# Heads by parity on the row halves, a four-block score product of 80 columns and a two-block one of 32

## Chip, cores and metric

The kernel runs on one core of a Trainium2 chip. The metric is the time of the whole program in microseconds (us) on that core. Everything is computed in float32.

## What is computed

```python
B, H, S, D = q.shape                         # 4, 8, 768, 48
mag = np.sqrt(a_re * a_re + a_im * a_im)
scale = np.minimum(mag, 0.999) / (mag + 1e-06)
a_re_n, a_im_n = (a_re * scale, a_im * scale)
for t in range(S):
    ...                                      # complex decay of the state S, then
    S_re, S_im = (new_re + kv, new_im)       # kv = outer(k_t, v_t)
    y[:, :, t] = q_t @ S_re
x = y.transpose(0, 2, 1, 3).reshape(B * S, H * D)    # 3072 x 384
h = np.maximum(np.maximum(x @ w1, x @ w2), x @ w3)   # 384 -> 768
return h @ w_out                                     # 768 -> 384
```

The recurrence is a gated linear attention with a complex decay for every head, step and feature. The kernel does it in tiles of 128 steps, each of two time chunks of 64: inside a chunk as a 64x64 lower-triangular matrix of scores per head, across chunks through a 48-feature complex state (96 rows of numbers, which lie in 112 rows: cosine parts in rows 0 to 47, nothing in 48 to 63, sine parts in 64 to 111).

## The kernel before

**Tiles.** A tile x is one sequence, 128 steps and all 8 heads; there are 24. Two tiles (two sequences, the same steps) make a group; there are 12. A tile's k, q and v lie as [128 rows, 2 chunks, 4 heads, 48]: rows 0 to 63 are the 64 steps of a chunk for heads 0 to 3, rows 64 to 127 the same steps for heads 4 to 7.

**Stages of a tile.** `gate_steps` and `angles` (ScalarE, VectorE, a little GpSimd) make the log-decays, cumulated phases, cosines and sines. `products` multiplies k and q by decay and phase into `uk` and `uq` (L471, L476, L481). `turn` transposes both with 16 matmuls against the identity, 64 rows at a time, and copies the results from PSUM on ScalarE into K (L495) and Q (L499). `cut` makes decay factors `f` at block borders: 16 small matmuls by a matrix of cuts, then four exponentials on ScalarE (L512 to L519). `prep` multiplies copies of K and Q by factors of f on VectorE (L527). `scores` makes two products on TensorE: A (K blocks of 32 keys x 48 columns of Q: the 32 queries of the block, and 16 more that carry a factor) and B (KB blocks of 32 keys x 80 columns of QB). `gather` assembles the 64x64 score matrices `atm` on VectorE with copies under a mask (L575): two from A, three from B. `state` carries the state on (`dk` on TensorE, L625 and L626 on VectorE). `outputs` sums "v times scores" and "state times q" into `y`, 32 output rows at a time, so that four runs go to four column strips of the array. Its result `xT` (L651) is what the feed-forward layer reads.

**Feed-forward.** `up_step` runs three weight matrices over 256 tokens and takes the maximum (L667, L669); `out_step` makes the 384 output columns and stores them (L677, L679).

**Layouts the change touches.** `vb` holds v as pairs of heads in 128 columns with a gap (a head in columns 0 to 47, the next in 80 to 127); each row half fills only its own four heads' slots and zeros stand in the others. So a 128-row product "v times scores" of two neighbouring heads' 32-row runs sees one head at a time: four runs of 32 for a pair, of which the two middle ones add into the same output strip. `g` (the state) has the same pairs. `uk` and `uq` have 128 columns per head.

**What sets the order.** TensorE's order is written out by hand from group 2 on: `chained` (L114) ties each matmul to the one before it in the source. ScalarE's table functions are tied in source order by `tab`. Everything else is ordered on each engine by the framework's planner, which lists instructions when it expects their inputs; the lists are fixed when the program is built. That it departs from the source can be seen in the trace. All loads and stores are issued on SP's queue. PSUM is a ring of four tiles of two banks (`banks`, L127), so a matmul group can wait for the reader of the tile four groups earlier.

In a group, after the first two tiles' prologue, the source order is:

```python
pairs(x)                     # scores A, B; gather A, B
turned(y)                    # turn k, q; cut; state; uk *= En; prep 0
outputs(x, tokens(x)); rest(y)
turning()                    # angles of the next group
pairs(y); units...; later    # uk, uq of the next group; gates of the one after it
turned(y + 1); outputs(y, tokens(y)); rest(y + 1)
```

with feed-forward steps of the tiles before fed in between by `feed`.

Of the kernel before, what the change touches and what calls it, by code (L numbers as in the profile page):

```python
# [51 lines left out]
def kernel(  # L52
# [31 lines left out]
    C8, C8B, C16, C32, CK, CG, CD, NF = 0, 4, 8, 12, 20, 28, 36, 37  # L84
# [83 lines left out]
    masko = const.tile([P, 4, 32], U8, name="masko")  # L168
# [4 lines left out]
    vbs = [const.tile([P, 2, H // 2, P], FP, name="vb%d" % i) for i in range(4)]  # L173
# [3 lines left out]
    us = {nm: [const.tile([P, H, 2, L64], FP, name="u%s%d" % (nm, i)) for i in range(n)] for nm, n in (("k", 3), ("q", 2))}  # L177
    fs = [const.tile([P, H, 2, NF], FP, name="f%d" % i) for i in range(2)]
    KB = const.tile([P, H, P], FP, name="KB")

    def constants_early():
# [11 lines left out]
        for o in (0, L64):  # L193
            def col(base, n):
                return cuts[o:o + L64, base:base + n]

            between(col(C8, 4), 7, 11, [[16, 4]], [[16, 4]])
            between(col(C8B, 4), 3, 7, [[16, 4]], [[16, 4]])
            vw = col(C16, 4).rearrange("p (n u) -> p n u", u=2)
            between(vw, 15, 19, [[32, 2], [0, 2]], [[32, 2], [8, 2]])  # L200
            vw = col(C32, 8).rearrange("p (i n) -> p i n", i=2)
            between(vw, 15, 35, [[16, 2], [0, 4]], [[0, 2], [8, 4]])
            vw = col(CK, 8).rearrange("p (n u) -> p n u", u=2)
            between(vw, 3, 15, [[16, 4], [8, 2]], [[16, 4], [0, 2]])
            between(col(CG, 8), -1, 3, [[0, 8]], [[8, 8]])

    def constants_late():
# [4 lines left out]
        f = nat1.tile([P, 4, 2, L64], FP, tag="e", padded_shape=[P, 6, 2, L64], name="maskf")  # L212
# [5 lines left out]
        g = f.rearrange("p i c t -> p (i c t)")[:, 0:4 * L64].rearrange("p (i t) -> p i t", i=4)  # L218
        nc.gpsimd.memset(g, 1.0)
        for i, h in enumerate((8, 16, 32, 32)):  # L220
            n, w = L64 // h, h if i < 2 else 16
            o = 16 if i == 3 else 0
            m = g[:, i].rearrange("p (n h) -> p n h", h=h)
            keep(m, -o, [[-2 * h, n], [0, h]], 1)
            keep(m, o + w - 1, [[2 * h, n], [0, h]], -1)
# [21 lines left out]
    def halves(a, g, c, j):  # L247
# [3 lines left out]
        return a[b * C + c, j * 4:(j + 1) * 4, t0:t0 + P, :].rearrange("h (c t) d -> t c h d", c=2)  # L251
# [8 lines left out]
    def load_v(g, c):  # L260
        x = g * C + c
        T["v", x] = vbs[x % 4]
        for j in range(2):
            src = halves(v, g, c, j).rearrange("t c (i u) d -> t c i u d", u=2)
            dst = T["v", x][j * L64:(j + 1) * L64, :, 2 * j:2 * j + 2]
            for ch in range(2):
                for u in range(2):
                    nc.sync.dma_start(out=heads(dst[:, ch])[:, :, u], in_=src[:, ch, :, u])
# [122 lines left out]
    def turns(g, cs, meanwhile):  # L391
# [8 lines left out]
        for c in cs:  # L400
            ps = banks("cs", DM)

            for ch in range(2):
                for j in range(2):
                    at = c * DM + j * HC
                    mm(out=ps[j * L64:(j + 1) * L64, ch * HC:(ch + 1) * HC], lhsT=upto[:, ch * L64:(ch + 1) * L64],
                       rhs=w[:, at:at + HC], start=True, stop=True)
# [7 lines left out]
            if (g + 1) % NS > 0:  # L415
                if c == 0:
                    T["carry", g + 1] = nat1.tile([1, W], FP, tag="carry", name="carry")
                for j in range(2):
                    last, at = (j + 1) * L64, c * DM + j * HC
                    nc.sync.dma_start(out=T["carry", g + 1][:, at:at + HC], in_=nf[last - 1:last, HC:])  # L420
# [20 lines left out]
    def both(t, h):  # L441

        return t[:, h].rearrange("p u d -> p (u d)")[:, 0:DD]
# [7 lines left out]
    def products(x):  # L451
        g, c = divmod(x, C)

        def s0():
# [3 lines left out]
            for n, mat in enumerate((mid, rest)):  # L458
                for j in range(2):
                    for ch in range(2):  # L460
                        r = slice(ch * L64, (ch + 1) * L64)
                        at = c * DM + j * HC
                        mm(out=ps[j * L64:(j + 1) * L64, ch, n * HC:(n + 1) * HC], lhsT=mat[r],
                           rhs=T["Ln", g][r, at:at + HC], start=True, stop=True)
# [8 lines left out]
        def s1():  # L473
            for nm in "kq":
                u = T["U" + nm, x] = us[nm][x % len(us[nm])]
                nc.vector.tensor_tensor(out=u[:, :, :, 0:D], in0=T["CS", x], in1=two(hd(T[nm, x])), op=OP.mult)  # L476

        def s2():

            u = T["Uk", x][:, :, :, 0:D]  # L480
# [5 lines left out]
    def turn(x, nm):  # L486
# [9 lines left out]
        else:  # L496

            T["Q", x] = un2.tile([P, 4 * H, 48], FP, tag="Q", name="Q")
# [3 lines left out]
    def cut(x):  # L502
# [3 lines left out]
        for i in range(2):  # L506
            for j in range(2):
                for u in range(2):
                    h, o = 4 * j + 2 * i + u, u * L64
# [11 lines left out]
    def prep(x, part):  # L521
# [12 lines left out]
        if part == 0:  # L534
            q8 = rows8(Q[:, :, 32:48])
            times(q8, base.rearrange("p g (n u e) -> p g n u e", u=2, e=8)[:, :, :, 1], C8, 4)
            times(q8, q8, C8B, 4)
        elif part == 1:

            times(*(rows8(t.rearrange("p s (j t) -> p (s j) t", j=2)[:, :, 0:48]) for t in (KB[0:DD], K)), CK, 6)  # L540

            QB = un1.tile([P, 2 * H, 96], FP, tag="QB", name="QB")
            T["KB", x], T["QB", x] = KB, QB
            ends = QB[0:DD].rearrange("p g (s u e) -> p g s u e", s=6, e=8)[:, :, 0::5]
            times(ends, rows8(base[:, :, 16:32]), C16, 4)
        elif part == 2:
            src = Q.rearrange("p (g j) t -> p g j t", j=2)[:, :, 1:2, 0:32].to_broadcast([DD, 2 * H, 2, 32])
            times(T["QB", x][0:DD, :, 16:80].rearrange("p g (i n e) -> p g i n e", i=2, e=8),
                  src.rearrange("p g i (n e) -> p g i n e", e=8), C32, 8)
# [6 lines left out]
    def scores(x, nm):  # L556

        ps = banks(nm)
        for h in range(H):
            for o in range(0, P, 32):  # L560
                c, j = divmod(o // 32, 2)
                if nm == "A":
                    mm(out=ps[o:o + 32, 0, h * 48:(h + 1) * 48], lhsT=T["K", x][0:DD, h, o:o + 32],
                                     rhs=T["Q", x][0:DD, 4 * h + 2 * c + j], start=True, stop=True)
                else:
                    mm(out=ps[o:o + 32, h // HU, h % HU * P:h % HU * P + 80],
                                     lhsT=T["KB", x][0:DD, h, o:o + 32],
# [309 lines left out]
```

## Time and profile before

| | before |
|---|---|
| time, median of 3 runs | 671.83 us (671.75 to 673.85) |
| profiled execution | 670.77 us, span 669.0 us |
| TensorE matmuls | 590.1 us busy, 88% |
| VectorE | 490.2 us busy, 73% |
| ScalarE | 389.5 us busy, 58% |
| GpSimd | 119.3 us busy, 18% |

A busy share says how much of the span an engine had work in flight. It is a mean over stages: until about 155 us the kernel loads and converts weights and starts up the first tiles, from then until about 600 us it repeats one group every 49.15 us, and at the end only the feed-forward of the last tokens is left. fp32 matmuls appear as two instructions each, transposes as one.

### The profile page before, as it was taken

The page shows a single profiled execution, that of the slowest core. Times are in us where ns is not written, and L with a number is a line of the kernel's source. Part 1 is how long each engine was busy: PE and PEld are TensorE (multiplying, and loading weights), DVE is VectorE, ACT ScalarE, POOL GpSimd, SP SyncE. Part 2 cuts the span into 40 slices and gives each one's busy share as a digit, 9 for nine tenths or more (in the row PEclk, how much of TensorE's full clock was granted, in tenths as well). Part 3 has the DMA queues.
Part 4 walks back from the last instruction along what each step waited for, and adds up shares of the span by engine and source line. Part 5 has one row for each costly group of instructions (what it writes and reads, how often), then busy time and mean ns, then how long its engine had stood idle before and what let it go on. Part 6 is the DMA issues. An engine that isn't in the chain of part 4 may idle for free.

```text
span 669.0 us, 25292 instructions
## 1 busy us (share of the span) xinstructions
PE 590.1 (88%) x11228; PEld 478.5 (72%) x11228; DVE 490.2 (73%) x662; ACT 389.5 (58%) x622; POOL 119.3 (18%) x126
## 2 busy tenths in 40 slices
PE   1254658898999999999999999999999999999997
PEld 0144656877867868867868878778778778888785
DVE  4899997987787787787777778787787778755111
ACT  6879686767665655665655755844944944430000
POOL 9400102305014014013023023023023023000000
PEclk9996987999999999999999999999999999999999
DMA  6584544330330430420420420321320210000000
GB/s 137 166 258 96 162 89 81 64 58 18 71 63 15 75 60 15 82 52 23 76 61 18 77 55 19 72 59 21 71 59 14 46 43 2 2 26 3 13 13 24
DMA packets 139052, 39.42 MB, mean 59 GB/s; under 512 B 131648, under 2 KB 134720, under 8 KB 138944
## 3 DMA queue, kind: packets, MB, share of 16 engines
q1 hardware_dynamic: 138944, 37.81, 26.0%
q8 instruction: 88, 1.44, 0.9%
q14 instruction: 20, 0.16, 0.1%
HBM read 33.03 MB, written 4.72 MB: 56 GB/s over the span
## 4 chain that ended last, share of the span: by engine, by line
PE 56%; ACT 21%; issue 8%; DVE 7%; DMA 3%; SPq 3%; POOL 1%; POOLq 0%; DVEq 0%; ACTq 0%
PE up L117 29%; PE op L117 13%; PE y L117 6%; ACT CS L112 2%; ACT L133 2%; ACT K L495 2%; ACT e L112 2%; PE B L117 2%; PE cs L117 2%; PE A L117 1%; SPq L258 1%; DVE Ln L369 1%; ACT L L112 1%; ACT f L112 1%; ACT w L112 1%
## 5 line engine op out<-in xcount | busy, mean ns | idle before, releaser
L117 PE MATMUL up<-xT,w 128*128 128x256 f32 (+1 forms) x1404 | 294.2, 367 | 8.7 <-ACT f L112 4.8
L117 PEld LDWEIGHTS up<-xT,w 128*128 128x128 f32 x1404 | 247.2, 190 | 45.4 <-ACT f L112 7.8
L117 PE MATMUL op<-wo,hT 128*128 128x384 f32 x288 | 100.2, 499 | 6.4 <-ACT K L495 6.4
L667 ACT COPY hT<-up 128x768 f32<-128x768 f32 (+2 forms) x27 | 19.6, 727 | 118.9 <-PE up L117 118.9
L117 PEld LDWEIGHTS op<-wo,hT 128*128 128x128 f32 x288 | 53.9, 193 | 41.8 <-ACT K L495 7.4
L669 DVE TENSOR_TENSOR hT<-hT,up 128x768 f32<-128x768 f32 (+2 forms) x54 | 46.4, 859 | 40.1 <-PE up L117 40.0
L527 DVE TENSOR_TENSOR Q<-Q,f 112x512 f32<-112x512 f32 x48 | 39.0, 813 | 49.0 <-ACT f L112 49.0
L379 POOL TENSOR_TENSOR ai<-ai,L 128x768 f32<-128x768 f32 x10 | 22.1, 2211 | 274.4 <-ACT L L112 248.9
L527 DVE TENSOR_TENSOR QB<-Q,f 112x512 f32<-112x512 f32 (+1 forms) x48 | 54.2, 1167 | 0.0
L117 PE MATMUL y<-atm,vb 128*32 128x64 f32 x1536 | 46.1, 228 | 4.7 <-DVE atm L575 4.7
L117 PEld LDWEIGHTS y<-atm,vb 128*32 128x32 f32 x1536 | 39.3, 114 | 14.1 <-issue 10.1
L117 PE MATMUL y<-QG,g 112*32 112x64 f32 x1408 | 44.9, 223 | 0.0
L112 ACT ACTIVATE f<-F 48x296 f32<-48x296 f32 x96 | 39.7, 413 | 0.9
L471 POOL TENSOR_TENSOR k<-E,k 128x384 f32<-128x384 f32 x20 | 25.9, 1293 | 74.3 <-ACT E L112 74.3
L117 PEld LDWEIGHTS y<-QG,g 112*32 112x32 f32 x1408 | 38.4, 113 | 0.0
L527 DVE TENSOR_TENSOR KB<-K,f 112x768 f32<-112x768 f32 x24 | 38.3, 1595 | 0.0
L481 DVE TENSOR_TENSOR uk<-uk,En 128x768 f32<-128x768 f32 x24 | 23.8, 993 | 16.9 <-PE tp L117 16.9
L117 PE MATMUL B<-QB,KB 112*32 112x80 f32 x1536 | 33.4, 242 | 2.1 <-DVE QB L527 2.1
L117 PE MATMUL sums<-Ln,mid 64*64 64x192 f32 x192 | 15.9, 362 | 21.9 <-DVE Ln L369 20.1
L387 POOL TENSOR_TENSOR ai<-ai,carry 1x768 f32<-1x768 f32 x10 | 18.6, 1861 | 88.0 <-ACT ai L384 81.8
L357 ACT ACTIVATE L<-ai 128x768 f32<-128x768 f32 (+1 forms) x13 | 10.3, 795 | 40.1 <-DVE w L380 28.3
L575 DVE COPY_PREDICATED atm<-masko,B 128x256 f32<-128x256 uint8 x72 | 31.6, 440 | 2.0
(104 smaller groups left out, 965.7 us busy)
## 6 DMA issues: line engine op xcount, KB each, us to landing
ar<-in_a_re_dram SPq DMA_DIRECT2D x24, 192.0 KB, 3.9
ai<-in_a_im_dram SPq DMA_DIRECT2D x24, 192.0 KB, 4.5
k<-in_k_dram SPq DMA_DIRECT2D x96, 48.0 KB, 2.5
q<-in_q_dram SPq DMA_DIRECT2D x96, 48.0 KB, 2.4
vb<-in_v_dram SPq DMA_DIRECT2D x192, 24.0 KB, 2.2
out_dram<-ot SPq DMA_DIRECT2D x24, 192.0 KB, 1.9
raw<-in_moe_w_dram SPq DMA_DIRECT2D x5, 768.0 KB, 5.2
w<-in_moe_w_dram SPq DMA_DIRECT2D x2, 768.0 KB, 5.9
```

Source lines behind the costliest of these rows:

```text
L112: tab(nc.scalar.activation(**kw))
L117: ins = f(**kw)
L133: tab(nc.scalar.preload_act_table_set(nm))
L379: (nc.gpsimd if g > 1 else nc.vector).tensor_tensor(out=ai, in0=ai, in1=L, op=OP.mult)
L387: nc.gpsimd.tensor_tensor(out=ai[0:1], in0=ai[0:1], in1=T["carry", g], op=OP.subtract)
L471: eng.tensor_tensor(out=hd(T[nm, x]), in0=E, in1=hd(T[nm, x]), op=OP.mult)
L481: nc.vector.tensor_tensor(out=u, in0=u, in1=two(T["En", x]), op=OP.mult)
L495: nc.scalar.copy(out=T["K", x][0:DD].rearrange("p n (j t) -> p j n t", j=2), in_=src)
L527: nc.vector.tensor_tensor(out=out, in0=in_, in1=f.to_broadcast([DD, 2 * H - g, n, 8]), op=OP.mult)
L575: nc.vector.copy_predicated(out=out, mask=mask, data=data)
L667: nc.scalar.copy(out=dst, in_=ps)
L669: nc.vector.tensor_tensor(out=dst, in0=dst, in1=ps, op=OP.max)
```

## The change

Heads go to the row halves by parity: rows 0 to 63 hold heads 0, 2, 4, 6 and rows 64 to 127 heads 1, 3, 5, 7. `vb` becomes 96 columns per pair without a gap, each row half filling its own head's 48, so that one 128-row product takes both heads of a pair in three 32-row runs. `uk` and `uq` shrink to 112 columns per head. Product A takes 80 columns of Q (the 32 own queries and 48 with factors), product B one 32-key block per chunk and 32 columns. `gather` now makes four masked copies from A (two before) and none from B (three before); B goes into `atm` by two plain copies on ScalarE, 32 rows each.

```diff
-    C8, C8B, C16, C32, CK, CG, CD, NF = 0, 4, 8, 12, 20, 28, 36, 37
+    C8, C16, CB, CK, C32, CG, CD, NF = 0, 4, 12, 18, 22, 26, 34, 35
...
-    masko = const.tile([P, 4, 32], U8, name="masko")
+    masko = const.tile([P, 3, 32], U8, name="masko")
...
-    vbs = [const.tile([P, 2, H // 2, P], FP, name="vb%d" % i) for i in range(4)]
+    vbs = [const.tile([P, 2, H // 2, 2 * D], FP, name="vb%d" % i) for i in range(4)]
...
-    KB = const.tile([P, H, P], FP, name="KB")
+    KB = const.tile([P, 2 * H, 32], FP, name="KB")
...
-        return a[b * C + c, j * 4:(j + 1) * 4, t0:t0 + P, :].rearrange("h (c t) d -> t c h d", c=2)
+        return a[b * C + c, j::2, t0:t0 + P, :].rearrange("h (c t) d -> t c h d", c=2)
...
-            src = halves(v, g, c, j).rearrange("t c (i u) d -> t c i u d", u=2)
-            dst = T["v", x][j * L64:(j + 1) * L64, :, 2 * j:2 * j + 2]
             for ch in range(2):
-                for u in range(2):
-                    nc.sync.dma_start(out=heads(dst[:, ch])[:, :, u], in_=src[:, ch, :, u])
+                nc.sync.dma_start(out=T["v", x][j * L64:(j + 1) * L64, ch, :, j * D:(j + 1) * D],
+                                  in_=halves(v, g, c, j)[:, ch])
+    def every(view, j):
+        return view.rearrange("p (i u d) -> p i u d", u=2, d=D)[:, :, j]
...
-                       rhs=w[:, at:at + HC], start=True, stop=True)
+                       rhs=every(w[:, c * DM:(c + 1) * DM], j), start=True, stop=True)
...
-                           rhs=T["Ln", g][r, at:at + HC], start=True, stop=True)
+                           rhs=every(T["Ln", g][r, c * DM:(c + 1) * DM], j), start=True, stop=True)
...
-            T["Q", x] = un2.tile([P, 4 * H, 48], FP, tag="Q", name="Q")
+            T["Q", x] = un2.tile([P, 4 * H, 80], FP, tag="Q", name="Q")
...
         if part == 0:
-            q8 = rows8(Q[:, :, 32:48])
-            times(q8, base...[:, :, :, 1], C8, 4)
-            times(q8, q8, C8B, 4)
+            times(rows8(Q[:, :, 48:64]), base...[:, :, :, 1], C8, 4)
+            times(two_, src, C16, 8)
+            times(rows8(Q[:, :, 48:72]), rows8(Q[:, :, 48:72]), CB, 6)
         elif part == 1:
-            times(*(... for t in (KB[0:DD], K)), CK, 6)
-            times(ends, rows8(base[:, :, 16:32]), C16, 4)
+            times(rows8(KB[0:DD]), rows8(K...[:, :, 0:32]), CK, 4)
         elif part == 2:
-            times(T["QB", x]..., src..., C32, 8)
+            times(rows8(QB[0:DD]), rows8(Q...[:, :, 1, 0:32]), C32, 4)
...
-                if nm == "A":
-                    mm(out=ps[o:o + 32, 0, h * 48:(h + 1) * 48], lhsT=T["K", x][0:DD, h, o:o + 32],
-                                     rhs=T["Q", x][0:DD, 4 * h + 2 * c + j], start=True, stop=True)
-                else:
-                    mm(out=ps[o:o + 32, h // HU, h % HU * P:h % HU * P + 80],
-                                     lhsT=T["KB", x][0:DD, h, o:o + 32],
-                                     rhs=T["QB", x][0:DD, 2 * h + c, 16 * j:16 * j + 80], start=True, stop=True)
+            if nm == "A":
+                for o in range(0, P, 32):
+                    mm(out=ps[o:o + 32, h // HU, h % HU * P:h % HU * P + 80], lhsT=T["K", x][0:DD, h, o:o + 32],
+                       rhs=T["Q", x][0:DD, 4 * h + o // 32], start=True, stop=True)
+            else:
+                for j in range(2):
+                    o = j * L64
+                    mm(out=ps[o:o + 32, 0, h * 32:h * 32 + 32], lhsT=T["KB", x][0:DD, 2 * h + j],
+                       rhs=T["QB", x][0:DD, 2 * h + j], start=True, stop=True)
...
-            pick(atm...[:, :, :, 1], over(masko[:, 1])..., src...[:, :, 0:5:4])
-            for i in range(2):
-                pick(atm[:, :, 32:], over(masko[:, 2 + i]), src[:, :, 16 + 32 * i:48 + 32 * i])
+            for i in range(2):
+                pick(atm...[:, :, :, 1], over(masko[:, 1 + i])..., own(32 + 32 * i, 16))
         else:
+            src = T[nm, x][:, 0, 0:H * 32].rearrange("p (h t) -> p h t", h=H)
+            for o in (0, L64):
+                nc.scalar.copy(out=atm[o:o + 32, :, 32:], in_=src[o:o + 32])
...
-                       rhs=T["v", x][r, ch, 2 * j + i // 2, o:o + D], start=True, stop=True)
+                       rhs=T["v", x][r, ch, i, j * D:(j + 1) * D], start=True, stop=True)
...
-                todo = [(n, new) for new in ((True, False) if x // C % NS > 0 or c > 0 else (True,)) for n in runs]
+                todo = [(V[:, c, i, 32 * w:32 * w + 32], atm[:, 4 * c + i])]
+                for n in ((0,), (1, 2), (3,))[w] if x // C % NS > 0 or c > 0 else ():
+                    todo.append((G[0:DD, c, i, 32 * n:32 * n + 32], QG[0:DD, 2 * (4 * c + i) + n // 2]))
```

Elsewhere the constants follow (cuts built with 16 ranges where there were 12, three masks where there were four, no zeroing of KB), the carry's last row goes out in four pieces of 48 numbers per transfer, and indices of heads follow the parity.

## Prediction

> **What bounds the kernel now.** I read the page's busy shares first, then the slices of the span, then who waited for whom on TensorE in the repeating part (205 to 620 us), then the order of time of one group.
>
> ```profile
> PE 590.1 (88%) x11228; PEld 478.5 (72%) x11228; DVE 490.2 (73%) x662; ACT 389.5 (58%) x622; POOL 119.3 (18%) x126
> ...
> PE   1254658898999999999999999999999999999997
> ...
> DVE  4899997987787787787777778787787778755111
> ```
>
> A slice is 16.7 us. TensorE (PE) is full from about the tenth slice on; in slices 3 to 6 VectorE (DVE) is. So the body belongs to TensorE and the prologue to VectorE. But a full slice still has holes:
>
> ```profile
> PE op L117 <- ACT K L495: 5.6, 7, 1.2
> PE up L117 <- ACT f L112: 2.7, 5, 0.7
> ```
>
> Seven times in that window (eight in the whole span) TensorE stands 1.2 us until ScalarE has copied K out of PSUM. The order of time of TensorE in one group shows where:
>
> ```profile
> 322.86 0.89 PE L117 MATMUL A<-Q,K 112*32 112x48 f32 x64
> 323.56 1.29 PE L117 MATMUL B<-QB,KB 112*32 112x80 f32 x64
> 324.78 8.04 PE L117 MATMUL up<-xT,w 128*128 128x256 f32 x36
> 332.75 0.66 PE L117 MATMUL tp<-ident,uk 64*112 64x64 f32 x16
> ...
> 336.11 4.14 PE L117 MATMUL op<-wo,hT 128*128 128x384 f32 x12 [1.21 <-ACT K L495]
> ```
>
> and ScalarE (ACT) in the same stretch:
>
> ```profile
> 331.40 0.92 ACT L368 ACTIVATE L<-L,biases 128x768 f32<-128x768 f32 x1
> 333.34 0.84 ACT L374 ACTIVATE e<-ar 128x768 f32<-128x768 f32 x1 [1.02 <-DVE Ln L369]
> 334.22 0.94 ACT L383 ACTIVATE ar<-ar,biases 128x768 f32<-128x768 f32 x1
> 335.06 0.99 ACT L495 COPY K<-tp 112x1024 f32<-112x1024 f32 x1
> ```
>
> The transposes of k are done at 333.41, yet K's copy starts at 335.06, behind L374 and L383, which belong to later gates. From the end of cs (322.9) ScalarE has only that one hole of 1.02 us. So each group of 49.15 us has two stretches: 13.2 us from cs to op that ScalarE ends, and 36 us from op to the next cs that TensorE ends, but for the 0.7 us on f.
>
> **What the skill says.** The Trainium skill, "TensorEngine Tiling (Array Packing)", Key Properties: tiles of the array load weights and multiply in parallel. The trace agrees: an A matmul lasts 206 ns, but 64 of them start within 0.70 us, 11 ns apart. The same page, PSUM Bottleneck: tiling speeds TensorE and not the emptying of PSUM, so use both ScalarE and VectorE for it; the change does, and here the stretch above speaks against it. "TensorE: Matmul & The Clock Gate", Architectural detail: ScalarE and VectorE are strictly first in, first out. The trace agrees (K's copy stood 1.65 us with its input ready). "VectorE: DVE Perf Modes", The TRN2 errata, prices an fp32 tensor_tensor at (N+151)/0.96 ns: 691 ns for 512; the undisturbed rows show 0.69 us.
>
> **The change part by part, per tile.**
>
> *Product A* goes from 48 to 80 columns. B has that shape now: its 64 instructions take 1.22 us (323.56 to 324.78) where A takes 0.70. So +0.52.
>
> *Product B* goes from 64 instructions of 80 columns to 32 of 32, on two column strips instead of four. Not shown. Low bound: A's 11 ns each, 0.35 us. High: strips half as many and weights not hidden, 22 ns each, 0.71. I take 0.5, A's rate scaled by columns and doubled for the strips (32/48 x 11 x 2 = 15 ns). So 1.22 to 0.5: -0.7 (-0.5 to -0.9).
>
> *y*: "v times scores" goes from 64 instructions to 48, "state times q" stays at 64. Today 128 take 1.95 us, 15.2 ns each; 112 take 1.71: -0.24.
>
> TensorE in all: -0.42 a tile, -10 us over 24. Strided moving operands in cs and sums, and narrower `uk` in the transposes: no row; 0 to +0.3 us a group if strides cost a tenth of cs and sums (3.3 us a group). I take 0.
>
> *VectorE, prep*: six multiplies before (512, 512, 768, 512, 1024, 1024 elements) and six after (512, 1024, 768, 512, 512, 1024): 4352 elements both times, so nothing. A now waits for three of them instead of two, +1.5 us; in the body Q's factors are ready at 338.6 and A starts at 346.2, so that is hidden; in the prologue A waited up to 6.1 us for Q, but B waited after it, for the same sum.
>
> *VectorE, gather*: five masked copies become four: -0.44 us (L575, 128x256). It is in slack in the body and on the bound in the prologue.
>
> *ScalarE, gather*: two copies of 32 rows x 256 from PSUM are new. Nearest row:
>
> ```profile
> L667 ACT COPY hT<-up 128x256 f32<-128x256 f32 x3 | 1.1, 364 | 0.0
> ```
>
> I take 0.37 each, 0.74 a tile (0.55 if they overlap by 0.1 as the E exponentials do, 0.8 by the f rows' 0.42). They write `atm`, so they wait for the four masked copies; behind them in ScalarE's queue stand the gates of the next groups, hT, K and Q. In tile x they fall into ScalarE's idle 2.5 us before hT (300.7 to 303.2): hidden. In tile y the fourth masked copy, by today's slots, ends at 328.7, amid the run of L112 rows that leads to L368, L374 and K: not hidden.
>
> *SP*: v takes 4 issues a tile instead of 8. A 24 KB issue holds the queue 0.60 us, k's 48 KB ones 0.65: -2.2 us a tile. The queue waits on others in the body, and vb is not what the prologue's VectorE waits for: 0. The carry's transfer in four pieces: its reader (L387) waits for ScalarE anyway: 0. GpSimd's start: 8 more selects at 0.22, two mask selects (0.4 each), KB's memset (0.3) and 0.9 us of vb's memset less: -0.2 us, 0, as cuts are used only at 35 us and are ready at 16.
>
> **The sum, against the profiled span of 669.0 (the three timed runs' median is 671.83; I subtract from that).** Stretch op to cs saves two y and one A+B: 0.48 + 0.2 = 0.68 a group, on TensorE's path. Stretch cs to op is ScalarE's: +0.74, and TensorE's 0.2 there is worth nothing. If that were all, a group would change by +0.06. But the planner sets ScalarE's list anew. It put K behind L383 and ahead of the next logarithm (L<-w), whose input is ready at 335.2; so it expected K's input between the start of L383 and about 1 us after. The new copies push L374 and L383 back by 0.74 and TensorE brings the transposes 0.2 us forward: 0.94 us, as much as L383 takes. So likeliest K moves ahead of L383. Then op starts 0.94 - 0.74 = 0.2 earlier, and a group saves 0.2 + 0.68 = 0.88; eight such groups 7.0. Outside them: the last four tiles, TensorE-bound, 4 x 0.42 = 1.7; four prologue tiles on VectorE 0.44 each less what waits elsewhere, 1.2. In all 9.9: **662**.
>
> **Rivals.**
>
> *ScalarE gives it back.* Order kept: +0.06 x 8 - 2.9 = -2.4, 669.4. For it: K's place behind L383 is the same in all eight groups. Against: the margin above is small.
>
> *K moves ahead of L374 too.* K copies at 333.2 and op waits for nothing: 1.2 + 0.2 + 0.68 = 2.1 a group, -16.7 - 2.9: 652. For: K has been earlier in the source than L374 all along. Against: needs a shift of 0.9 to 2 us.
>
> *Slower: ScalarE stalls on the masked copies.* If the two plain copies are listed right behind the table load (328.17) while VectorE still strews its masked copies between the multiplies of uk and uq (today the last ends at 329.9), everything behind them, K too, stands up to 1.7 us and then 0.74: (2.4 - 0.68) x 8 - 2.9 = +10.9, 682; half the stall gives 676. It decides from 1.3 us a group (0.68 + 2.9/8 + 0.3). Against: the planner lists VectorE from the same expectations.
>
> The change does what it says by its text: instruction counts follow from the loops.
>
> **Chances.** K ahead of L383: 0.40. Ahead of both: 0.15. Given back: 0.23, half of it within 0.3% (2.0 us, about what a measurement of this kernel tells from no change). Stall: 0.22, of which some ends within. So faster 0.63, same 0.15, slower 0.22. The range leaves out the end of the stall and a little of the fast case: 652 to 676. The likeliest case by itself, with B and the strides at their bounds and the prologue's lists moved by 3 us, would be 657 to 667.
>
> **What would show it.** A at 19 to 20 ns a start, B's 32 instructions in about 0.5 us, y in 1.7; two new ScalarE rows of about 0.37 us, 48 in all; no L575 row that reads B; K's place in the list from cs to op, and the wait of op on K (1.2 now; 1.1 to 1.2 forecast, 2.1 if given back, 0 in the fast case); a group of 48.3 us instead of 49.15. Wrong if B takes over 0.7 us, if ScalarE waits for atm's masked copies, or if the prologue (until 155 us) moves by more than 3 us.

## The result, and the profile after

| | before | after |
|---|---|---|
| time, median | 671.79 us (4 runs, 670.53 to 673.85) | 668.0 us (4 runs, 667.46 to 668.85) |
| profiled execution, span | 669.0 us | 666.7 us |

The ratio is 0.9942 with a 95% interval of 0.9914 to 0.997: 3.8 us faster, where 9.9 was forecast. The sign was right and the size was not.

The page of the changed kernel: engine, busy us, share of the span, instructions; then the busy tenths in 40 slices.

```profile
PE 581.8 (87%) x10076; PEld 472.5 (71%) x10076; DVE 476.9 (72%) x638; ACT 404.2 (61%) x670; POOL 122.4 (18%) x131
...
PE   1244777898999999999999999999999999999997
...
DVE  3899998985777877877776687778778777655111
```

TensorE has 1152 matmul records fewer and lost 8.3 us of work, VectorE 13.3 us; ScalarE went from 389.5 to 404.2 us. The shape over the slices is the same: a prologue of VectorE, then TensorE nearly full. So the question is again which wait ends last in the stretch from cs to op. Who waited for whom on TensorE, 205 to 620 us (us in total, times, longest us):

```profile
PE dk L117 <- DVE hT L676: 4.8, 7, 0.7
PE up L117 <- ACT f L112: 3.9, 8, 0.6
PE up L117 <- DVE g L633: 3.6, 6, 0.6
PE op L117 <- ACT K L501: 0.4, 1, 0.4
```

Op's wait on K is gone. The last number of such a row is the longest wait and not each one: before the change the row read 5.6 us in seven times, and six of the seven were 0.74 us. TensorE in a group before, and two lines of the group that the prediction shows:

```profile
285.08 1.14 PE L117 MATMUL dk<-vb,uk 64*64 64x48 f32 x64
286.96 4.14 PE L117 MATMUL op<-wo,hT 128*128 128x384 f32 x12 [0.74 <-ACT K L495]
...
334.23 0.68 PE L117 MATMUL dk<-vb,uk 64*64 64x48 f32 x32
336.11 4.14 PE L117 MATMUL op<-wo,hT 128*128 128x384 f32 x12 [1.21 <-ACT K L495]
```

In the second, 32 of dk's 64 records are missing from the trace, and the gap looks 0.47 us longer; the 0.4 us that is left after the change stands in such a group too.

In the place of that wait dk waits 0.7 us for hT, seven times, and there is a wait that the kernel before hasn't: `up` 0.6 us for `g`, six times. Two orders of time show the two places. TensorE from cs to op (start, us, engine line, operation, shape):

```profile
276.57 1.31 PE L117 MATMUL A<-Q,K 112*32 112x80 f32 x64
277.70 0.68 PE L117 MATMUL B<-QB,KB 112*32 112x32 f32 x32
278.31 8.04 PE L117 MATMUL up<-xT,w 128*128 128x256 f32 x36
...
288.56 1.14 PE L117 MATMUL dk<-vb,uk 64*64 64x48 f32 x64 [0.68 <-DVE hT L676]
289.63 4.14 PE L117 MATMUL op<-wo,hT 128*128 128x384 f32 x12
```

and ScalarE in the same stretch:

```profile
282.63 0.72 ACT L603 COPY atm<-B 32x256 f32<-32x256 f32 x2
...
285.73 0.92 ACT L370 ACTIVATE L<-L,biases 128x768 f32<-128x768 f32 x1
287.67 0.84 ACT L376 ACTIVATE e<-ar 128x768 f32<-128x768 f32 x1 [1.02 <-DVE Ln L371]
288.54 1.01 ACT L501 COPY K<-tp 112x1024 f32<-112x1024 f32 x1
289.45 0.94 ACT L385 ACTIVATE ar<-ar,biases 128x768 f32<-128x768 f32 x1
```

A's 64 instructions start within 1.13 us, B's 32 within 0.61 (277.70 to 278.31); the two copies of B take 0.72 together and stand in the run of gates that leads to K; K's copy is now ahead of the sign instruction L385 (L383 before). So op starts 14.51 us after the start of cs, 14.71 before.

**Where the time went.** From the start of one cs to the next is one group. This splits the spans; each kernel has two traces (the second pair are experiments 11 and 12):

| us | before | after | mean change | forecast |
|---|---|---|---|---|
| start to the fourth cs | 172.69, 174.16 | 177.23, 175.19 | +2.8 | -1.2 |
| fourth to twelfth cs, eight groups | 394.03, 392.76 | 389.39, 389.38 | -4.0 | -7.0 |
| twelfth cs to the end | 102.28, 102.38 | 100.08, 100.13 | -2.2 | -1.7 |

The tail is near the forecast, the groups gave a little over half of theirs, and the prologue went the other way. One group blurs the split: in the first trace of the kernel before, the one that starts at the fourth cs lasted 50.40 us, in the second 49.19. Counted to the fifth cs the change costs 1.9 us, and the seven groups from there take 343.63 and 343.57 us before, 340.44 in both traces after: 0.45 us a group less.

**The new wait.** In a group's other half the `up` products come in two rows with y between them. The second row takes the PSUM tile that `dk` held, and dk's last reader is VectorE's last addition to the state, `g<-g,dk`. VectorE before:

```profile
258.23 0.69 DVE L527 TENSOR_TENSOR Q<-Q,f 112x512 f32<-112x512 f32 x1 [2.67 <-ACT f L112]
258.84 0.55 DVE L626 TENSOR_TENSOR g<-g,dk 112x384 f32<-112x384 f32 x1
259.31 1.41 DVE L527 TENSOR_TENSOR Q<-Q,f 112x512 f32<-112x512 f32 x1
260.64 1.35 DVE L625 TENSOR_TENSOR g<-g,f 112x384 f32<-112x384 f32 x1
261.92 1.75 DVE L527 TENSOR_TENSOR KB<-K,f 112x768 f32<-112x768 f32 x1
263.59 0.54 DVE L626 TENSOR_TENSOR g<-g,dk 112x384 f32<-112x384 f32 x1
```

and after:

```profile
260.65 0.69 DVE L533 TENSOR_TENSOR Q<-Q,f 112x512 f32<-112x512 f32 x1 [2.61 <-ACT f L112]
261.26 0.55 DVE L633 TENSOR_TENSOR g<-g,dk 112x384 f32<-112x384 f32 x1
261.72 1.95 DVE L533 TENSOR_TENSOR Q<-Q,f 112x1024 f32<-112x1024 f32 x1
263.60 1.35 DVE L632 TENSOR_TENSOR g<-g,f 112x384 f32<-112x384 f32 x1
264.87 1.76 DVE L533 TENSOR_TENSOR Q<-Q,f 112x768 f32<-112x768 f32 x1
266.55 0.54 DVE L633 TENSOR_TENSOR g<-g,dk 112x384 f32<-112x384 f32 x1
```

Two multiplies stand between the first addition and the last in both. Before they have 512 and 768 elements (1.41 and 1.75 us), after 1024 and 768 (1.95 and 1.76). From the start of the first `up` (258.25 and 260.67) to the end of the last addition it is 5.88 us before and 6.42 after. The second `up`:

```profile
258.25 4.15 PE L117 MATMUL up<-xT,w 128*128 128x256 f32 x18 [0.51 <-ACT f L112]
...
264.28 8.04 PE L117 MATMUL up<-xT,w 128*128 128x256 f32 x36
```

```profile
260.67 4.15 PE L117 MATMUL up<-xT,w 128*128 128x256 f32 x18 [0.44 <-ACT f L112]
...
267.15 8.04 PE L117 MATMUL up<-xT,w 128*128 128x256 f32 x36 [0.60 <-DVE g L633]
```

It started 6.03 us after the first before, and 6.48 now. Before the change the addition ended 0.15 us ahead of `up` (264.13 and 264.28; in the second trace 0.15 us in five of the eight groups and 0.29 in a sixth). That is a chain with hardly any slack, and the view of waits doesn't show it. y's saving of 0.24 us meets it even without longer multiplies, as experiment 3 shows.

The multiplies take this long while GpSimd multiplies E by k and q in the same stretch (261.6 to 267.5). The Trainium skill, "SBUF — State Buffer", Summary: rules for kernel authors, says that of a VectorE operation with two SBUF inputs and a GpSimd operation that reads SBUF, the second to issue is blocked until the first is finished. The trace agrees in size: GpSimd's first product ends at 262.59, and the 1024-element multiply, which takes 1.22 us where it runs by itself, ends 1.08 us after that, at 263.67. In experiment 5 it again ends 1.08 us after a product of GpSimd (264.98 and 266.06). No run takes GpSimd's products away, so the cause of the length is read from these times and not shown by an experiment.

### The profile page after: what moved, and what is told of

Read it like the earlier page. It is cut to its first block, busy times and chain, and to the rows that moved or that the text cites. A ratio compares the mean times of both kernels' runs of the same rounds, so it can differ in the third digit from the quotient of the medians.

```text
span 666.7 us, 22815 instructions
## 1 busy us (share of the span) xinstructions
PE 581.8 (87%) x10076; PEld 472.5 (71%) x10076; DVE 476.9 (72%) x638; ACT 404.2 (61%) x670; POOL 122.4 (18%) x131
## 4 chain that ended last, share of the span: by engine, by line
PE 46%; ACT 24%; DVE 16%; issue 8%; DMA 3%; SPq 2%; POOL 1%; DVEq 0%; POOLq 0%; ACTq 0%
PE up L117 24%; PE op L117 12%; DVE Q L533 6%; PE y L117 3%; ACT CS L112 3%; ACT f L112 2%; ACT L133 2%; ACT e L112 2%; PE A L117 2%; ACT Q L505 2%; PE cs L117 2%; ACT K L501 2%; PE dk L117 2%; DVE g L632 2%; DMA ai<-in_a_im_dram 1%
## 5 line engine op out<-in xcount | busy, mean ns | idle before, releaser
L533 DVE TENSOR_TENSOR Q<-Q,f 112x512 f32<-112x512 f32 (+2 forms) x72 | 91.6, 1278 | 49.2 <-ACT f L112 49.2
L117 PEld LDWEIGHTS op<-wo,hT 128*128 128x128 f32 x288 | 53.2, 190 | 34.9 <-DVE hT L676 0.8
L117 PE MATMUL A<-Q,K 112*32 112x80 f32 x1536 | 34.7, 247 | 12.8 <-DVE Q L533 12.8
L117 PEld LDWEIGHTS A<-Q,K 112*32 112x32 f32 x1536 | 29.9, 117 | 21.8 <-issue 13.6
L117 PE MATMUL y<-atm,vb 128*32 128x64 f32 x1152 | 39.5, 224 | 0.9 <-issue 0.7
L117 PEld LDWEIGHTS y<-atm,vb 128*32 128x32 f32 x1152 | 32.6, 112 | 10.4 <-issue 5.6
L112 ACT ACTIVATE f<-F 48x280 f32<-48x280 f32 x96 | 38.3, 399 | 0.9
L117 PE MATMUL y<-QG,g 112*32 112x64 f32 x1408 | 38.3, 220 | 0.0
L477 POOL TENSOR_TENSOR q<-E,q 128x384 f32<-128x384 f32 x20 | 34.9, 1747 | 0.0
L117 PE MATMUL cs<-w,upto 128*64 128x192 f32 x192 | 20.1, 355 | 15.7 <-DVE w L400 15.7
L412 DVE SCALAR_TENSOR_TENSOR nf<-t,cs 128x384 f32<-128x384 f32 x24 | 13.3, 554 | 28.5 <-ACT t L410 27.4
```

The source lines that it names most:

```text
L112: tab(nc.scalar.activation(**kw))
L117: ins = f(**kw)
L477: eng.tensor_tensor(out=hd(T[nm, x]), in0=E, in1=hd(T[nm, x]), op=OP.mult)
L533: nc.vector.tensor_tensor(out=out, in0=in_, in1=f.to_broadcast([DD, 2 * H - g, n, 8]), op=OP.mult)
```

## The experiments

Numbers 3, 4, 10 and 15 are edits of the kernel before, numbers 1, 2, 5 to 9, 13 and 14 of the changed kernel. Numbers 1 to 7, 9, 10, 13 and 14 are set against the kernel before run beside them (671.7 to 672.0 us); 8, 11, 12 and 15 are single executions with a trace.

**1. The long multiplies to the end.** Part 0 keeps only the 512-element multiply; the other two move to part 2, behind QB's.

```diff
         if part == 0:
             times(rows8(Q[:, :, 48:64]), ..., C8, 4)
-            times(two_, src, C16, 8)
-            times(rows8(Q[:, :, 48:72]), rows8(Q[:, :, 48:72]), CB, 6)
...
         elif part == 2:
             times(rows8(QB[0:DD]), ..., C32, 4)
+            times(two_, src, C16, 8)
+            times(rows8(Q[:, :, 48:72]), rows8(Q[:, :, 48:72]), CB, 6)
```

> The changed kernel with two of prep's multiplies moved: part 0 keeps only the first (512 elements), and the two large ones (1024 and 768) come after those of KB and QB. Same work. Theory 1 (the large multiplies stand on VectorE between the state's additions, whose PSUM tile the next up matmuls need): TensorE's wait of 0.60 us of up on g, six times in the body, goes, VectorE's list from Q to the last addition of the state gets some 0.8 us shorter, the group falls by 0.4 to 0.6 us and the whole by 3 to 5 us. Theory 2 (ScalarE's list alone decides the group): the wait moves elsewhere and the time stays within 1 us. Rival (planner's noise in the prologue is all there is): the body's group stays at 48.94 us.

Measured: 672.83 us, ratio 1.0009 (0.9998 to 1.002). A miss: 4.8 us slower than the changed kernel. Its trace is experiment 8.

**2. B's copies on VectorE.**

```diff
-                nc.scalar.copy(out=atm[o:o + 32, :, 32:], in_=src[o:o + 32])
+                nc.vector.tensor_copy(out=atm[o:o + 32, :, 32:], in_=src[o:o + 32])
```

> The changed kernel with the two plain copies of B on VectorE instead of ScalarE. Theory 2 (the two copies, 0.74 us, lie in ScalarE's run from cs to op and delay the log-decay on VectorE, hT, dk and K): Ln, hT and dk come 0.7 us earlier after cs and dk's wait of 0.68 us on hT goes; but if K goes back behind the sign instruction L385, op still starts 13.2 us after cs instead of 13.06, and the time moves by -1 to +2 us. If K stays ahead of it: -0.6 us a group, -5 us. Theory that ScalarE's copies cost nothing: no change in the body, and + 1 us in the prologue, since VectorE gets 0.78 us a tile more.

Measured: 668.32 us, 0.9943 (0.9925 to 0.9961), the same as with ScalarE; a group of 49.13. On TensorE, 205 to 620 us:

```profile
PE op L117 <- ACT K L501: 5.6, 7, 1.2
...
PE up L117 <- DVE g L633: 3.6, 6, 0.6
```

K went back behind L385 and op waits for it as before the change: without the two copies the planner keeps the old order, so K's turn follows from their 0.74 us, as the prediction argued. What ScalarE saved, the order took back.

**3 and 4. Each half of the change by itself.** Number 3 has only the heads by parity (with v in 96 columns and the shorter y), number 4 only the new scores, prep and gather (with the narrower uk and uq).

Number 3's edit and then number 4's, both on the kernel before:

```diff
-    vbs = [const.tile([P, 2, H // 2, P], FP, name="vb%d" % i) for i in range(4)]
+    vbs = [const.tile([P, 2, H // 2, 2 * D], FP, name="vb%d" % i) for i in range(4)]
...
+                todo = [(V[:, c, i, 32 * w:32 * w + 32], atm[:, 4 * c + i])]
```

```diff
-            T["Q", x] = un2.tile([P, 4 * H, 48], FP, tag="Q", name="Q")
+            T["Q", x] = un2.tile([P, 4 * H, 80], FP, tag="Q", name="Q")
...
+                nc.scalar.copy(out=atm[o:o + 32, :, 32:], in_=src[o:o + 32])
```

> The kernel before with heads by parity, the 96-column v and the shorter y, and the old scores, prep and gather. TensorE saves 0.24 us a tile in y. Theory 1: in tile x the up after y then meets the state's last addition (which ended 0.1 us before y did), so only 0.1 of the 0.24 counts there; tile y counts in full: 0.34 us a group, 2.7 us, and 1 us in the tail: 3 to 4 us less than before. If TensorE alone decided: 0.48 a group, 5 us less. If the loss of the changed kernel's prologue (4.4 us by the start of the second repeating group) came from the parity layout: no gain or a loss.

> The kernel before with the new scores, prep and gather (and the narrower uk and uq, which make room), heads in the old order and the old y. Theory 1 and 2 together: A and B save 0.2 us a group, K's turn 0.2, the state's addition behind the large multiplies takes 0.2 to 0.5 back, so the group stays within 0.2 us of 49.15; the prologue carries the loss of some 4 us; in all 0 to 5 us slower than before. If TensorE alone decided: 0.4 us a group less, 3 to 5 us faster.

Measured: 668.87 us for number 3, 0.9957 (0.9941 to 0.9972), a group of 48.84; 669.95 for number 4, 0.9966 (0.9955 to 0.9978), a group of 49.15. Number 3 came out as forecast (3.1 us for 3 to 4, 0.31 a group for 0.34), and its trace shows the chain without slack: in six of eight groups the second `up` starts 0.05 us after the state's last addition and 1.86 us after the start of y, which takes 1.73 where nothing holds what follows. What a typical group gains comes with the parity. The new scores, 0.18 us a tile less on TensorE, leave it where it was, as was said of number 4; in number 4's trace `up` waits for `g` too (1.5 us in four times). Its total came out 2 us below the kernel before, where 0 to 5 above was expected; in the trace the tail is 1.2 us shorter than in the mean of the two traces before, the eight groups 1.5 us shorter (391.85), and the start to the fourth cs 2.5 us longer, so that this one trace shows only 0.3 of the 2 us.

**5. The state's last addition first.** In tiles from 4 on, the 1024-element multiply is ordered behind it.

```diff
+            last = T.get("added")
...
-            times(two_, src, C16, 8)
+            ins = times(two_, src, C16, 8)
+            if T.pop("added", None) is not None and x > 3:
+                tc.add_manual_dep(ins.ins, last.ins.name, order, reason="state first")
```

> The changed kernel with one thing more: where a state addition comes before a tile's second multiply of part 0 (from tile 4 on), that multiply (1024 elements) is ordered behind the state's last addition. ScalarE's list in the repeating part stays as in the changed kernel. Theory 1 (the enlarged part 0 stands ahead of the state's last addition, which alone lets go of dk's PSUM tile, and the next up products wait for it): the waits of 0.60 us for g in tile x go, the leg from the first up's start to the second falls from 6.48 to about 6.0 us, a group lasts 48.3 to 48.6 us instead of 48.94, and the whole is 3 to 5 us faster than the changed kernel (668.0), 663 to 665. Theory 2 (that wait is only where another limit shows, GpSimd's products that slow VectorE or ScalarE behind them): the wait reappears under another name within the same group and the group stays within 0.2 us of 48.94, the whole within 1.5 us of 668.

Measured: 663.52 us, 0.9872 (0.9854 to 0.9891); a group of 48.27, and from the first `up` to the second 5.80 us (6.48). The fourth cs to the twelfth takes 385.82 us, 3.6 less than in the changed kernel and 7.6 less than before. VectorE:

```profile
260.02 1.41 DVE L533 TENSOR_TENSOR KB<-K,f 112x512 f32<-112x512 f32 x1
261.35 1.35 DVE L635 TENSOR_TENSOR g<-g,f 112x384 f32<-112x384 f32 x1
262.62 1.48 DVE L533 TENSOR_TENSOR QB<-Q,f 112x512 f32<-112x512 f32 x1
264.03 0.54 DVE L636 TENSOR_TENSOR g<-g,dk 112x384 f32<-112x384 f32 x1
264.49 1.57 DVE L533 TENSOR_TENSOR Q<-Q,f 112x1024 f32<-112x1024 f32 x1
```

With the 512-element KB and QB between them (1.41 and 1.48) the additions are done at 264.57, and `up` starts at 264.77 without a wait. The first theory holds, with its number (663 to 665 us and 48.3 to 48.6 a group were forecast).

**6. The gates of group 2 later**, to keep the prologue's masked copies from standing behind a subtraction.

```diff
-          (0.75, 1.0, gate_steps(2, list(range(C)))))
+          (0.75, 1.0, gate_steps(2, list(range(C)))[:2]))
...
-        if g > 1:
-            gates[2]()
+        gates[2]()
```

> The changed kernel with the third step of group 2's gates called in group 1 after its first scores, as for the later groups, and not at the end of the prologue. Prologue theory (in group 1's second tile VectorE's masked copies stand behind the subtraction L383 that waits for GpSimd's L381, the new copies of B on ScalarE wait for them, and hT, K, Q and the rows of f behind these): with the subtraction listed behind the masked copies, TensorE's waits of 1.78 us (tp of q on atm) and 0.81 us (F on atm) in that tile go and the distance from the start of the third cs to that of the fourth falls from 49.5 to some 47 us: 2 to 4 us less in all, 664 to 666. Rival (the prologue is bound by VectorE's sum of work, and a moved step only moves the wait): within 1 us of 668. The repeating part stays at 48.94 us a group in both.

**7. Experiments 5 and 6 together.**

> Both edits of the two runs before together (state's last addition first; third step of group 2's gates later). If both theories hold they add: 3 to 5 and 2 to 4 us, 659 to 663, and it would beat both kernels. If only the first holds, 663 to 665; if only the second, 664 to 666; if neither, 668.

Measured: 667.25 us (0.9931, 0.9916 to 0.9947) and 663.7 (0.9874, 0.9856 to 0.9892): the step brings nothing that can be told. In the trace of number 6 the waits of 1.78 and 0.76 us are still there. The subtraction in their way is that of group 3's gates, in tile 4, which this edit doesn't move: the place was wrong, so the theory wasn't tested. Experiment 13 does.

**8. Number 1 once more, for its trace.**

> The kernel of the first experiment again, for its trace. Whether its 4.8 us more than the changed kernel lie in the groups (then a group lasts about 49.5 us, and the product A should be seen to wait for the multiply of Q that is now listed behind L382 and L383 or behind the second QB), or in the prologue (then groups at about 48.5 us, as the first theory has it, and the fourth cs starts near 186 us instead of 177).

Measured: a group of 49.72 us. The wait on `g` is gone, as the first theory has it, but

```profile
PE A L117 <- DVE Q L533: 4.4, 7, 1.2
PE dk L117 <- ACT hT L674: 1.3, 5, 0.3
```

In that kernel VectorE's list has both long multiplies after QB, and the second of them behind L382 (248.61 in the group from 224.79). A starts 0.46 us late for it, everything after A too, and the copies of B then push hT on ScalarE. So it lies in the groups. "A's third multiply is hidden", as the prediction had it, is true only of the place where the change puts it.

**9. K and the maximum first**, on top of number 5.

```diff
-            nc.vector.scalar_tensor_tensor(out=part("Ln"), ...)
+            ins = nc.vector.scalar_tensor_tensor(out=part("Ln"), ...)
+            if g > 2:
+                tc.add_manual_dep(ins.ins, T["max"].ins.name, order, reason="maximum first")
...
-            nc.scalar.activation(out=e, in_=ar, func=AF.Abs)
+            ins = nc.scalar.activation(out=e, in_=ar, func=AF.Abs)
+            if g > 2:
+                tc.add_manual_dep(ins.ins, T["Kcopy"].ins.name, order, reason="K first")
...
+        feed(2)
         for f in later:
             f()
-        feed(2)
```

> The kernel of the fifth experiment (state's last addition first) with two more orders set for the repeating part: K's copy ahead of ScalarE's L376, and the last maximum of hT ahead of VectorE's Ln (L371), for which the four up products are called before those gates. By the trace of that kernel: dk no longer waits 0.69 us for hT nor op 0.37 for K, so op starts 1.06 us earlier after cs (13.45 us instead of 14.51), and ScalarE's f is ready some 1.3 us earlier, so that the 0.5 us wait of up on f goes too. If the stretch from cs to op is then TensorE's alone: a group of 46.7 to 47.2 us instead of 48.27 and 651 to 656 us in all. If the waits only change their names: 48.0 to 48.3 a group and 661 to 664.

**10. The same two orders on the kernel before.**

> The kernel before with the same two orders (K's copy ahead of its L374, last maximum ahead of Ln at its L369), without anything of the change. Its group has waits of 1.21 us (op on K) and 0.70 us (up on f): if both go, 47.2 to 47.5 us instead of 49.15, and 656 to 660 us in all. It tells what the change is worth where ScalarE doesn't end the stretch from cs to op: by TensorE's terms (A, B and y, 0.42 us a tile forecast) the kernel of the run before this one should be 0.7 to 1.0 us a group faster than this one; if ScalarE's two new copies still cost something, the difference is smaller, down to 0.

Measured: 656.04 us (0.9767, 0.9743 to 0.9791) and 664.04 us (0.9884, 0.9861 to 0.9906). Number 9 beats both kernels: a group of 47.38, op 13.62 us after cs, and of the waits from 205 to 620 us one kind is left:

```profile
PE up L117 <- ACT f L112: 4.0, 8, 0.6
```

Both forecasts were too good, number 10's by 4 us. The wait on f is that of the group's other half, where neither edit is, and stays; and on the kernel before op starts 0.90 us earlier (13.81 us after cs) where number 10 had counted on 1.21: what it had waited was 0.74, and the other 0.16 lies in dk ahead of it. In the same way number 9 had counted the 0.37 us of the group with missing records, and op came 0.89 us earlier instead of 1.06. Number 10's groups are read from number 15, which is the same kernel.

**11 and 12. Both kernels once more.**

> The kernel before once more, for a second trace of its prologue. If the 4.5 us that the changed kernel's fourth cs starts later are all the change's, the fourth cs starts here at 172.2 to 173.2 us as in the first trace. If part of them is how one execution differs from another (the first cs alone lay between 25.9 and 27.4 us in executions with the same code up to there), it starts later, at 173.5 to 175.5.

> The changed kernel once more, for a second trace of its prologue: its fourth cs at 177 us if the first trace is typical, at 175 to 176.5 if that one was slow. Groups of 48.94 us in both cases.

Measured: the fourth cs at 174.16 and 175.19 us, the groups as in the first traces. So of the 4.5 us between the first two traces about 1.7 were how executions differ, and the change costs the prologue 2.8 (1.0 to 4.5 by which traces are paired), or 1.9 (0.8 to 3.1) when it is counted to the fifth cs.

**13. Masked copies ahead of the subtraction, in tile 4 alone.**

```diff
-            nc.vector.scalar_tensor_tensor(out=w, in0=w, scalar=2.0, in1=ai, ...)
+            ins = nc.vector.scalar_tensor_tensor(out=w, in0=w, scalar=2.0, in1=ai, ...)
+            if g == 3:
+                tc.add_manual_dep(ins.ins, T["pick"].ins.name, order, reason="masked copies first")
```

> The changed kernel with one order set, for one tile only (tile 4, at 150 to 157 us): the subtraction L383 of group 3's gates behind that tile's four masked copies. If the hold on A's and B's PSUM tiles costs the prologue its time: TensorE's waits of 1.78 us (tp of q on atm) and 0.81 us (F on atm) fall to at most 0.5 together, the third distance between cs starts falls from 48.7 to 49.5 us to about 47, and the whole is 1.5 to 2.5 us faster than the changed kernel (668.0): 665.5 to 666.5. If VectorE's sum of work binds, the waits go and others come in the same stretch: 667 to 668.5. Groups stay at 48.94 us.

**14. That order on number 9.**

> The kernel with the state's last addition, K and the maximum first (656.0) and the order of the run before this one too. 653.5 to 654.5 if that order saves 1.5 to 2.5 us in the prologue, 655 to 656.5 if it doesn't.

Measured: 667.01 us (0.9923, 0.9905 to 0.9941) and 654.42 us (0.974, 0.9718 to 0.9763): 1.0 and 1.6 less than without it, with intervals that overlap. The first lies where the rival put it (667 to 668.5), the second where the theory did (653.5 to 654.5). What they aim at, in the changed kernel, TensorE:

```profile
156.24 0.66 PE L117 MATMUL tp<-ident,uq 64*112 64x64 f32 x16 [1.78 <-DVE atm L579]
157.71 0.87 PE L117 MATMUL F<-cuts,Ln 64*48 64x35 f32 x32 [0.81 <-ACT atm L603]
```

and in number 13 (who waited for whom, 126 to 178 us):

```profile
PE dk L117 <- ACT hT L676: 1.1, 1, 1.1
PE F L117 <- ACT atm L605: 0.9, 1, 0.9
```

Four masked copies now read A's PSUM tile where two did, and two of the four stood behind L383, which waits for GpSimd; so tp waited 1.78 us for that tile (0.53 before). F's wait is not new (0.84 before, on a masked copy). With the order set tp's wait is gone, F's on the copies of B stays, and dk takes over with 1.1 us on hT. In number 13 the wait mostly changes its name; whether the order is worth anything, these two times don't tell.

**15. The trace of number 10's kernel.**

> The kernel before with K and the maximum first, for a trace at full clock. From its time (664.0) and the second trace of the kernel before a group should last 49.15 - 7.7/8 = 48.2 us, and the kernel of the ninth experiment (47.38) is then 0.8 us a group faster: TensorE's 0.84 a group as forecast. If ScalarE's two new copies still cost in that kernel, this one's group is 47.4 to 47.9.

Measured: a group of 48.25 us against 47.38 in number 9: 0.87.

## Why the prediction was right in sign and wrong in size

**TensorE's terms: right.** A took 1.13 us (1.22 forecast), B 0.61 (0.5), together 1.74 against 1.72; y 1.72 (1.71). Where only the wait on f is left besides TensorE's own work, the change saves 0.87 us a group by experiments 9 and 15, and 0.84 was the sum of these terms.

**ScalarE and K's turn: right.** The two copies take 0.72 a tile (0.74), K moved ahead of the sign instruction and no further, and op came 0.20 us earlier, to the digit. What the forecast didn't name is who ends the stretch: not K but dk, on hT, whose maximum stands behind Ln on VectorE. Both chains hang on the same ScalarE run and end together (K's copy at 289.55, op starts behind dk at 289.63), so the size held, and that the second chain ended level with the first was luck. One reading was wrong: "seven times ... TensorE stands 1.2 us" took the longest wait for each, and it was 0.74. The sum of 9.9 doesn't use it, but the rival in which K passes L374 as well does: its 1.2 us was too large, and with the maximum left where it is dk would still have stood. Experiment 9 moves both and brings 0.9. (With half of "given back" counted, its chances of "faster" add up to 0.67 and not 0.63.)

**The step that failed: "VectorE, prep: six multiplies before and six after, 4352 elements both times, so nothing".** The sum was right and the place was not asked for. The part that grew (1024 elements for 512) stands between the state's additions, the last of which lets go of dk's PSUM tile. It had 0.15 us of slack, and now holds `up` 0.60 us in six of eight groups: 3.6 us. Of each 0.60 about 0.1 is y's saving meeting the chain (0.13 in experiment 3) and the rest the longer multiplies. Experiment 5 takes the wait away, gets 3.6 us back in the groups and makes a group last 48.27 us, 0.88 less than before, which is the forecast's own sum. The forecast asked of the added element work who waits for A, and of the removed wait who waits for K; it did not ask what else was queued behind the longer multiplies.

**The second term: "four prologue tiles on VectorE 0.44 each less what waits elsewhere, 1.2".** It was -1.2 and measured +2.8. VectorE did save: from the first cs to the fourth it is busy 132.4 and 132.5 us before, 130.3 and 130.5 after. But it ends only part of that stretch. Most of the loss lies between the third cs and the fourth (46.93 and 46.91 us before, 49.46 and 48.69 after), and there TensorE has more work than VectorE. The stretch in the first trace of each kernel, before and after (window and its length; busy us of TensorE, its weight loads, VectorE, ScalarE and GpSimd; granted clock, DMA share, GB/s):

```profile
125.76:172.69 46.93, 43.29 (x954) 36.33 (x955) 39.00 (x52) 29.42 (x47) 9.71 (x6) 1.00 0.28 52
127.77:177.23 49.46, 45.56 (x858) 38.23 (x858) 36.37 (x49) 31.04 (x51) 10.79 (x6) 0.93 0.28 53
```

TensorE's busy time rose by 2.3 us with 96 records fewer (by 1.1 in the second traces, 43.14 to 44.23), and its idle time by 0.3 and 0.7. So slower matmuls at a lower granted clock (1.00 in both traces before, 0.93 and 0.96 after) are a rival that no experiment tests; the clock alone doesn't settle it, as the kernel of number 15 read 0.96 there and took 47.08. Of the forecast's own rival, "ScalarE stalls on the masked copies", tile 4 shows the late masked copies, once, and not in the groups; the one that stands is TensorE, while ScalarE's copies of B follow L387 without a gap. Taking that hold away gave back 1.0 us at most in the changed kernel. From the first cs to the second (51.7 us before, 53.2 after in the mean, 51.4 and 51.2 with one half of the change) neither half alone loses anything, yet by the fourth cs each is late (175.24 and 175.90; 173.4 before in the mean). What of the 2.8 us comes from VectorE's list, what from the clock and what from chance in two traces each, stays open.

**Tail: right** within 0.5 us (-2.2 for -1.7). Its split over the terms is not shown: the parity alone shortens the tail by 0.2 us and the scores alone by 1.2.

Put together: forecast -9.9; the wait on `g` takes 3.6 of the groups' share and the prologue 4.0 (2.8 where -1.2 was forecast); the rest is within 1.2 us of the traces' -3.5.

## What to carry to other kernels

An equal sum of work is not no change: ask for each instruction that grows what stands behind it in its engine's list, and which buffer the next one there lets go of. A chain that ended just in time shows in no view of waits; before claiming a saving on one engine, measure how early the other engines' last reader of each PSUM tile was done. And if an edit brings less than its sum, the repair may be one order: here three orders set on top of it were worth more (12.0 us, 668.0 to 656.04) than the change (3.8). Two of them are worth 7.7 us on the kernel before as well, and with all three the changed kernel is 8.0 us ahead of that one. And a row of waits gives a total, a count and the longest: divide before using it, and look whether the group of the longest has all its records.

## What the runs showed of the hardware

- VectorE's multiplies beside GpSimd's took longer than by themselves: 1.95 us where 1.22 (1024 elements), 1.76 to 2.57 where 0.95 (768). The longest ended 0.81 us after GpSimd's operation beside it (345.21 and 346.02), another 0.82 us after (296.81 and 297.63).
- From the fifth cs to the twelfth, seven groups repeat between two executions to 0.06 us in the kernel before (343.63 and 343.57) and to 0.01 in the changed one. The fourth cs differs by 1.5 and 2.0 us (172.69 and 174.16, 177.23 and 175.19), and the group after it by 1.2 us in the kernel before.
- The granted clock is not 1.00 throughout in the prologue: from the third cs to the fourth it read 1.00 in both traces before, 0.93 and 0.96 in the two after. Small matmuls in tile 4 show it: the 32 of F took 0.87 us in the first trace after, 0.57 in the second and in both before. What lowers it there, these runs don't show.
